# Float16 stacks with a per-row scale for the masked scores, and stacks of two head pairs on chip

## The chip, the cores and the metric

The kernel runs on one core of one Trainium2 chip. The metric is the device time of one execution in microseconds (us): the median of the runs of a kernel. The profile shows one execution, taken by the hardware profiler.

## The reference

The input is `q`, `k`, `v` of 4 batches, 8 heads, 768 rows and 64 columns, a projection of 64x6, and the weights of a two-layer block (512 to 2048 to 512). Cut to what matters:

```python
q_bucket = sum over n of (q @ proj[:, n] > 0) * 2**n        # 6 bits, and the same for k
mask     = q_bucket[:, :, :, None] == k_bucket[:, :, None, :]
scores   = where(mask, (q @ k^T) / 8, -1e9)                  # 768 x 768 for each head
attn     = exp(scores - rowmax); attn /= rowsum + 1e-9
x        = (attn @ v), heads side by side                    # 3072 x 512
h        = maximum(x @ w_in, 0)
out      = (h * h) @ w_out
```

## The kernel before

**Units and visits.** A unit is 128 rows of scores of one head against all 768 keys; there are 192 units (lines 840 to 848). A visit is six units: one half (384 rows) of a pair of heads, three units of each head. There are 32 visits, eight for each batch. The first eight visits (batch 0, 48 units) are "plain": their scores are one product of float32 stacks. The other 144 units (batches 1 to 3) work with two products of float32r stacks, and these are the ones that the change touches.

**Stacks.** `prep` (line 582) makes the operands of one pair of heads. `R` is loaded with 64 rows of k above 64 rows of q. A projection gives `pd`, the sign of it the bits (`bits`, ScalarE), and a small matmul turns these into bit patterns (`pc`). `A` is `R` rounded to float32r, with q scaled by 1/8; `L` is the rest that the rounding left out. Five DMAs from SBUF to SBUF on SP's queue (`send`) rearrange the halves, so that the first product (`Q` with `A`) and the second (`M` with `L`) add up, in PSUM, to the full-precision score and to the mask: the bit rows lie in `M`, with values of the order of 2^100, so that a row whose bits differ falls out of the exponential. Each of `A`, `L`, `Q`, `M` is 128x768 of 4 bytes in two buffers (line 37). A pair of heads takes one buffer of each for each head, so both buffers are taken by one pair, and a head of the next pair waits until the same head of the pair before has been read for the last time.

**One unit** (line 671). TensorE writes four score matmuls into `pS` (two products, two halves of 384 columns). From unit 36 on `pS` has one place in PSUM only: every second unit before that uses the space of `po` (line 674). VectorE takes the negated row maximum `nmx` (line 682). ScalarE writes `e = exp(pS + nmx)` with the row sum `sm` (line 685). Then `rv = 1/(sm + 1e-9)` (VectorE or GpSimd, then a reciprocal on VectorE), `hl` is `e * rv` split into two float16 parts (the high part mostly on ScalarE, the low part on VectorE), a DMA transpose writes `aT`, and `av` (line 709) multiplies it with the values, `pA`. `pS` comes free for the next unit when the exponential has read it.

**The two-layer block** (`moe`, line 732) runs for each half batch as soon as its four visits are done: 16 steps `f` with 12 matmuls `pm` (384 columns) and 9 matmuls `po` (512 columns) each. ScalarE and VectorE turn `pm` into the two float16 parts of `g`. It is what TensorE has to do beside the units.

**The order** of all instructions is made by a list scheduler in the kernel itself (`Program.order`, line 238): every operation is recorded with its cost (line 188), the scheduler runs forward and backward a few times, and the result is what each engine executes in order. `rank` is its first priority. `PACE` (line 64) holds the matmuls of the two-layer block back: the step number m may not start before the unit that is read off between the points (unit, step), so that at unit 193 step 640 of 896 is allowed. All instructions are issued by one helper, so that nearly all have line 420 (and 417 for grouped matmuls) in the profile; one goes by the tiles' names.

Of the kernel before, what the change touches and what calls it, by code (L numbers as in the profile page):

```python
# [30 lines left out]
NF = DFF // P  # L31
BIG = float(2.0**100)
SC = 0.125
ASC = float(2.0**14)


# [24 lines left out]
WIN_AT, WOUT_AT = (0, 2), 1  # L61
FIRST = len(WIN_AT)

PACE = ((25, 0), (64, 120), (193, 640))

IDLE_FROM, IDLE_SHARE = 1000, 0.6

# [55 lines left out]
class Program:  # L123
# [35 lines left out]
    def add(self, *ways):  # L159


        ways = [w for w in ways if w[0].key != "pool" or not any(isinstance(x, View) and x.rec.kind == "psum" for x in w[2])]
        queue, name, args, kw = ways[0]
        if name == "matmuls":
            used = [(x, n == 0) for a, _ in args for n, x in enumerate(a)]
        else:
            used = [(args[0], True)] + [(x, False) for x in args[1:]] + [(x, k == "accum_out") for k, x in kw.items()]
        used = [(x.rec, w, self.region(x)) for x, w in used if isinstance(x, View)]
        i, deps = len(self.ops), set()
        for rec, w, (p0, p1, f0, f1, fs, g0, g1) in used:  # L170
            if rec.before is not None:
                deps |= rec.before.ops
            for j, w2, (a0, a1, b0, b1, bs, c0, c1) in rec.accesses:
                if (w or w2 or rec.kind == "psum") and a0 < p1 and p0 < a1 and b0 < f1 and f0 < b1 and not (fs and fs == bs and (c1 <= g0 or g1 <= c0)):
                    deps.add(j)
        for rec, w, r in used:
            rec.ops.add(i)
            rec.accesses.append((i, w, r))
        deps.discard(i)
        if self.mark is not None:  # L180
            self.paced.append((i, self.mark))
        behind = () if name == "matmuls" or not name.startswith("dma") or queue.key != "sp" else self.first
        self.ops.append(Op([w + (self.cost(w[0].key, *w[1:]), self.port(w[0].key, *w[1:])) for w in ways], deps, self.rank))
        if i not in behind:
            self.ops[i].after |= set(behind)

    @staticmethod
    def cost(key, name, args, kw):

        size = lambda x: int(np.prod(x.shape[1:]))  # L190
        column = {F32: 4 / 2.4, F32R: 0.445}
        if name == "matmuls":

            side = {32: 4, 64: 2}.get(size(args[0][0][1]), 1)
            t = sum(size(a[2]) * column.get(a[2].dtype, 1 / 2.4) + 7 for a, _ in args) / side
            return t, t
        kinds = [x.rec.kind if isinstance(x, View) else "" for x in args]
        ptr = any(isinstance(x, View) and x.shape[-1] == 1 for x in args[2:3])
        n = max(size(args[0]), size(args[1]) if isinstance(args[1], View) else 0)
        if key == "pe":  # L200
            if "is_transpose" in kw:
                return 110, 110
            t = max(107, size(args[2]) * column.get(args[2].dtype, 1 / 2.4) + 3)
            return t, t
        if name.startswith("dma"):
            b = int(np.prod(args[0].shape)) * mybir.dt.size(args[0].dtype)
            inside = name == "dma_start_transpose" or kinds[:2] == ["sb", "sb"]
            busy = 1040 if key == "pool" else (650 if inside else 475) + 50 * (key == "act")
            return busy, b / (TRANSPOSES if name == "dma_start_transpose" else 314)
        if key == "act":  # L210
            t = 93 * (isinstance(kw.get("scale"), View) + isinstance(kw.get("bias"), View)) + (51 if "psum" in kinds[:2] else 93) + n / 1.2 + 93 * ("accum_out" in kw)
        elif key == "pool":
            t = 147 + n * (2.1 if args[0].dtype == F32 or args[0].dtype == F32R else 1.88) if name == "tensor_tensor" else 161 + n / 1.2 + 83 * ptr
        else:
            fast = name in ("tensor_copy", "tensor_scalar") and "psum" not in kinds[:2]
            both = len(args) > 3 and isinstance(args[3], View) and args[3].shape[-1] == 1
            t = 67 + n / (1.92 if fast else 0.96) + 62 * (ptr and (fast or name == "scalar_tensor_tensor")) + 100 * both
        return t, t
# [8 lines left out]
    @staticmethod  # L227
    def port(key, name, args, kw):

        if name.startswith("dma") or key not in ("dve", "pool"):  # L230
            return False
        ins = [x for x in args[1:] if isinstance(x, View) and x.shape[-1] > 1]
        inside = all(x.rec.kind == "sb" for x in ins)
        if key == "pool":
            return any(x.rec.kind == "sb" for x in args[1:] if isinstance(x, View) and len(x.shape) > 1 and x.shape[-1] > 1)
        return inside and (len(ins) == 2 or name in ("tensor_copy", "tensor_scalar"))
# [157 lines left out]
    def emit(self):  # L394
        info = mybir.DependencyInfo(mybir.DependencyClass.NoSync, mybir.DependencyReason.DATA)
        last = {}
        def issue(q, ins):
            if q.key in last:
                self.tc.add_manual_dep(ins, last[q.key], info, reason="in order")
            last[q.key] = ins.name  # L400
        out = self.order()
        fill, end = {}, IDLE_FROM
        for i in out[: out.index(self.busy_from)]:
            o = self.ops[i]
            if o.queue is self.pe:
                if o.start > end + 300:
                    fill[i] = int((o.start - end) * IDLE_SHARE / 56)
                end = o.start + o.busy
        for i in out:
            o = self.ops[i]  # L410
            q = o.queue
            for _ in range(fill.get(i, 0) if self.idle[1].rec.tile is not None else 0):
                issue(q, q.engine.matmul(self.idle[0].real(), self.idle[1].real(), self.idle[1].real(), start=True, stop=True).ins)
            real = lambda x: x.real() if isinstance(x, View) else x
            if o.name == "matmuls":
                for args, kw in o.args:
                    ins = q.engine.matmul(*map(real, args), **kw).ins  # L417
                    issue(q, ins)
                continue
            ins = getattr(q.engine, o.name)(*map(real, o.args), **{k: real(x) for k, x in o.kw.items()}).ins  # L420
            issue(q, ins)

# [10 lines left out]
def lsh_attention_moe(ctx: ExitStack, tc, kq, v, proj2, w_in, w_out, consts, out):  # L433
# [27 lines left out]
    def sb(shape, dtype, name, bufs=1, tag=None):  # L461
        return pr.tile(sbp, "sb", shape, dtype, name, BUFS.get(tag or name, bufs), tag)
# [116 lines left out]
    def matmuls(*args, start=True, stop=True):  # L579
        pr.add((pe, "matmuls", [(a, {"start": start, "stop": stop}) for a in args], {}))  # L580

    def prep(b, hp, plain):
        r0 = pr.rank
        Rs, Rqs = [], []
# [14 lines left out]
        matmuls(*[(pd[32 * n : 32 * n + 32], pj, Rs[n // 2][:, n % 2 * HS : (n % 2 + 1) * HS]) for n in range(4)])  # L599
        bits = sb([P, HS], BF16, "bits")  # L600
        act.activation(bits, pd, AF.Sign, scale=2.0**60, bias=thr)
        out = []
        for odd, R in enumerate(Rs):
            pr.rank = r0
            if plain:
                M = sb([P, S], F32, "M" if odd else "L")
            else:

                A, L, Q, M = [sb([P, S], F32R, name) for name in "ALQM"]
                move(A, R, cst[:, 2:3])  # L610
                left(L, R, cst[:, 2:3], f32(A))
            pr.rank = r0 + STACKS
            if not plain:
                send(f32(Q[T]), f32(A[U]))
                send(f32(Q[U]), f32(L[U]))
                send(f32(A[U]), f32(A[T]))
            for half in range(2):
                w = slice(half * HS, (half + 1) * HS)
                n = 2 * odd + half
# [3 lines left out]
            if plain:  # L623

                move(R[U], M[T], 1.0, HALVES if r0 > 0 else (act, dve))
                move(M[T], Rqs[odd], SC)
                out.append(((M, R),))
            else:
                send(f32(L[U]), f32(M[T]))
                send(f32(M[T]), f32(Q[T]))  # L630
                out.append(((Q, A), (M, L)))
        return out

    vscales, loaded = {}, {}
# [36 lines left out]
    def unit(st, half, i, aT, plain):  # L671
# [6 lines left out]
            for j in range(2):  # L678
                pe.matmul(pS[:, j, 0:HS], a[:, c0 : c0 + P], bb[:, j * HS : (j + 1) * HS], start=s == 0, stop=s == len(st) - 1)
        sS = pS[:, 0:2, 0:HS]  # L680
        nmx = sb([P, 1], F32, "nmx", 2)
        dve.tensor_reduce(nmx, sS, AX.XY, ALU.max, negate=True)
        e = sb([P, S], F32, "e", BUFS["e"])
        sm = sb([P, 1], F32, "sm", 2)
        act.activation(e.rearrange("p (j s) -> p j s", j=2), sS, AF.Exp, bias=nmx, accum_out=sm)
        pr.rank = u
        rv = sb([P, 1], F32, "rv", 3)
        pr.add(*[(q, "tensor_scalar", (rv, sm, 1e-9, 1.0 if plain else 1.0 / ASC, ALU.add, ALU.mult), {}) for q in (dve, pool)])
# [35 lines left out]

    def unscaled(b, j=None):

        back = sb([P, 1], F32, "back", 16)
        dve.tensor_scalar(back, vscales[b][1], vscales[b][1], 2.0**46, ALU.mult, ALU.mult)
        dve.tensor_scalar(back, back, common if j is None else zs[:, j : j + 1], 1.0, ALU.mult, ALU.mult)
        return back  # L730
# [167 lines left out]
```

## Time and profile before

| what | us |
|---|---|
| median of 3 runs | 894.41 (893.44 to 894.41) |
| the profiled execution | 897.11 |
| its span in the profile | 895.3 |
| first and last exponential of the 144 float32r units | 193.7, 766.0 |
| last but one | 732.1 |

The span falls into four stretches. Up to 194 us the plain units run and the weights are split. From 194 to 732 us the 143 units of batches 1 to 3 run, with the two-layer block of the half batches before them. From 732 us on it is nearly the two-layer block alone, with one last unit at 766 us. In the tables of the profile PE is TensorE's matmuls, PEld its weight loads, DVE is VectorE, ACT ScalarE, POOL GpSimd. A group's row gives its busy time and the mean duration of one in ns; matmuls overlap in the pipeline, so the mean of one is longer than the time from one to the next. In a timeline a row stands for the first of its instructions, with start, time and count.

### The profile page before, as it was taken

How to read it: one execution, taken by the hardware profiler on the slowest of the kernel's cores; microseconds unless marked ns; L12 is line 12 of the kernel's file. 1: busy time of each engine (PE TensorE's matmuls, PEld its weight loads, DVE VectorE, ACT ScalarE, POOL GpSimd, SP SyncE). 2: the span in 40 equal slices, each digit the busy share in tenths (PEclk: the TensorE clock that was granted, in tenths of full speed). 3: DMA queues.
4: the chain of work that ended last, by engine and by line, in shares of the span. 5: the costliest groups of instructions: out<-in, count | busy, mean ns of one | idle time of the engine just before them, and what ended most of it. 6: DMA issues, size and time to landing. Idle time of an engine off the chain costs nothing.

```text
span 895.3 us, 14201 instructions
## 1 busy us (share of the span) xinstructions
PE 860.8 (96%) x5082; PEld 478.9 (53%) x5082; DVE 612.0 (68%) x1149; ACT 641.3 (72%) x1180; POOL 110.5 (12%) x159
## 2 busy tenths in 40 slices
PE   7997988999999999999999999999999999999997
PEld 5553543455555555555555555555555555555553
DVE  5888888989888677888776768887767661211111
ACT  4877786889798778798777868877778773533433
POOL 2663653300220000100000000000000000000000
PEclk9998997999999999999999999999999999999999
DMA  7548549787989897999898968897979740200000
GB/s 239 174 127 170 169 154 236 160 176 150 209 180 205 140 203 132 221 186 211 153 216 151 201 125 186 171 183 130 184 146 202 146 89 17 73 1 1 36 0 36
DMA packets 279974, 131.82 MB, mean 147 GB/s; under 512 B 258272, under 2 KB 258400, under 8 KB 279904
## 3 DMA queue, kind: packets, MB, share of 16 engines
q1 hardware_dynamic: 279424, 130.91, 69.2%
q8 instruction: 40, 0.66, 0.3%
q14 instruction: 30, 0.25, 0.1%
q10 hardware_dynamic: 480, 0.01, 0.0%
HBM read 37.30 MB, written 6.29 MB: 49 GB/s over the span
## 4 chain that ended last, share of the span: by engine, by line
PE 46%; DMA 2%; ACT 2%; DVE 2%; issue 1%; SPq 0%; ACTq 0%
PE po L420 18%; PE pm L420 17%; PE pS L420 6%; PE pA L417 5%; DMA M<-Q 1%; ACT o L420 1%; DVE nmx L420 1%; ACT g L420 1%; ACT hl L420 0%; DMA L<-M 0%; DMA Q<-L 0%; PE pd L417 0%; DVE hl L420 0%; ACT e L420 0%; PE pc L420 0%
## 5 line engine op out<-in xcount | busy, mean ns | idle before, releaser
L420 PE MATMUL pm<-xx,win 128*128 128x384 f16 x1536 | 330.2, 328 | 1.8 <-ACT g L420 1.6
L420 PE MATMUL po<-wo,g 128*128 128x512 f16 x1152 | 330.0, 380 | 0.9 <-ACT o L420 0.8
L420 DVE TENSOR_REDUCE nmx<-pS 128x1 f32<-128x768 f32 x192 | 183.1, 953 | 54.3 <-PE pS L420 52.0
L420 ACT ACTIVATE e<-pS,nmx 128x768 f32<-128x768 f32 x192 | 172.0, 896 | 64.0 <-DVE nmx L420 59.1
L420 PEld LDWEIGHTS <-win 128*128 128x128 f16 x1536 | 145.7, 98 | 119.2 <-issue 20.6
L420 DVE SCALAR_TENSOR_TENSOR hl<-e,rv,hl 128x768 f16<-128x768 f32 x162 | 164.6, 1018 | 30.0 <-ACT hl L420 29.7
L420 PEld LDWEIGHTS <-g 128*128 128x128 f16 x1152 | 107.5, 98 | 127.5 <-issue 21.6
L420 ACT ACTIVATE hl<-e,rv 128x768 f16<-128x768 f32 x157 | 145.3, 929 | 24.3 <-ACT e L420 12.1
L420 DVE SCALAR_TENSOR_TENSOR g<-g,g 128x384 f16<-128x384 f32 x122 | 67.5, 554 | 129.1 <-ACT g L420 128.3
L420 ACT ACTIVATE g<-pm 128x384 f32<-128x384 f32 x125 | 60.8, 486 | 103.3 <-PE pm L420 103.1
L420 ACT ACTIVATE g<-g 128x384 f16<-128x384 f32 (+1 forms) x251 | 130.4, 520 | 5.7 <-PE po L420 0.6
L420 PE MATMUL pS<-A,Q 128*128 128x384 f32 x288 | 93.1, 403 | 5.7 <-ACT e L420 5.7
L417 PE MATMUL pA<-aT,VV 128*64 128x384 f16 x972 | 91.6, 329 | 0.0
L420 POOL TENSOR_SCALAR rv<-sm 128x1 f32<-128x1 f32 x71 | 27.3, 384 | 482.1 <-ACT e L420 480.3
L420 PE MATMUL pS<-L,M 128*128 128x384 f32 x288 | 76.5, 346 | 1.6 <-DMA M<-Q 1.6
L417 PEld LDWEIGHTS <-VV 128*64 128x64 f16 x972 | 49.4, 109 | 37.7 <-issue 19.7
L420 PEld LDWEIGHTS pS<-A,Q 128*128 128x128 f32 x288 | 47.4, 189 | 34.0 <-ACT e L420 20.7
L420 PEld LDWEIGHTS pS<-L,M 128*128 128x128 f32 x288 | 51.5, 188 | 5.3 <-issue 3.2
L420 PE MATMUL pS<-Q,M 128*128 128x384 f32 x96 | 39.3, 526 | 4.6 <-ACT e L420 4.6
L420 PE MATMUL pS<-A,L 128*128 128x384 f32 x96 | 38.8, 519 | 4.2 <-ACT e L420 4.2
L420 DVE TENSOR_SCALAR rv<-sm 128x1 f32<-128x1 f32 x121 | 18.3, 151 | 32.1 <-ACT e L420 29.0
L420 DVE TENSOR_SCALAR M<-pc,cst 128x384 fp32r<-128x384 f32 (+1 forms) x56 | 37.6, 671 | 2.5 <-PE pc L420 2.4
(111 smaller groups left out, 679.5 us busy)
## 6 DMA issues: line engine op xcount, KB each, us to landing
R<-kq SPq DMA_DIRECT2D x24, 384.0 KB
raw<-w_in SPq DMA_DIRECT2D x16, 511.8 KB
raw<-w_out SPq DMA_DIRECT2D x16, 511.8 KB
V<-vp SPq DMA_DIRECT2D x16, 384.0 KB
out<-o SPq DMA_DIRECT2D x21, 256.0 KB
Q<-L SPq DMA_DIRECT2D x24, 192.0 KB
Q<-A SPq DMA_DIRECT2D x24, 192.0 KB
A<-A SPq DMA_DIRECT2D x24, 192.0 KB
```

The source lines that it names most:

```text
L417: ins = q.engine.matmul(*map(real, args), **kw).ins
L420: ins = getattr(q.engine, o.name)(*map(real, o.args), **{k: real(x) for k, x in o.kw.items()}).ins
```

## The change

Stacks are float16. For each pair of heads a new function `bounded` finds from the sums of squares of `R` (two ScalarE squares with accumulated sums, a small matmul `pn`, nine small VectorE operations) a power of two for k and q, `own`, by which `A` is scaled before it is rounded to float16, and `exact`, the factor that turns the product back. The mask values become 49152 in place of 2^100, which `cst` and `sgn` are rescaled for once. The exponential then has a scale for each row: `exact`, or 0 for a row whose maximum tells that no key has the same bits. So for each of the 144 units VectorE runs two more operations on 128x1 behind the row maximum, in one piece (`chain`), and the exponential reads its scale and its bias from SBUF.

`A` and `Q` of a head are now the halves of one tile of 128x2x768 float16, `L` and `M` those of another; the first head of a pair takes the tags `A` and `L`, the second `Q` and `M`. A tile has the bytes of one before, each tag still has two buffers, and a pair of heads takes one buffer of each, so that two pairs are on chip. The five DMAs for each head move half the bytes. `PACE` allows step 680 at unit 193, and `back` has 12 buffers in place of 16.

```diff
-PACE = ((25, 0), (64, 120), (193, 640))
+PACE = ((25, 0), (64, 120), (193, 680))
...
+            if o.name == "chain":
+                for name, args, kw in o.args:
+                    issue(q, getattr(q.engine, name)(*map(real, args), **{k: real(x) for k, x in kw.items()}).ins)
+                continue
...
+    def bounded(Rs):
+
+        if not halved:
...
+            dve.tensor_scalar(cst[:, 0:2], cst[:, 0:2], fac, 1.0, ALU.mult, ALU.mult)
...
+        sums = sb([P, 2], F32, "sums")
+        for n, R in enumerate(Rs):
+            act.activation(sb([P, S], BF16, "sqk", tag="sqv"), R, AF.Square, accum_out=sums[:, n : n + 1])
+        for n, h in enumerate((T, U)):
+            dve.tensor_scalar(few[h, 2 * n : 2 * n + 2], sums[h], 2.0**120, 1.0, ALU.min, ALU.mult)
+        pn = ps([P, 512], F32, "pn", tag="misc")[:, 0:4]
+        pe.matmul(pn, ones, few, start=True, stop=True)
+        both = sb([P, 8], F32, "both")
+        size, flip = both[:, 0:4], both[:, 4:8]
+        dve.tensor_scalar(size, pn, 2.0**8, 2.0**120, ALU.max, ALU.min)
+        dve.tensor_scalar(u32(size), u32(size), 1, 0x7F800000, ALU.logical_shift_right, ALU.bitwise_and)
+        dve.tensor_scalar(u32(flip), u32(size), 0x7F800000, 0x7F800000, ALU.bitwise_xor, ALU.bitwise_and)
+        found = sb([P, 4], F32, "found", 4)
+        own, exact = found[:, 0:2], found[:, 2:4]
+        for n, h in enumerate((T, U)):
+            dve.tensor_scalar(own[h], flip[h, 2 * n : 2 * n + 2], 2.0**-51, 1.0, ALU.mult, ALU.mult)
+        dve.tensor_scalar(size, size, 2.0**50, 1.0, ALU.mult, ALU.mult)
+        dve.scalar_tensor_tensor(exact, size[:, 0:2], SC, size[:, 2:4], ALU.mult, ALU.mult)
+        return own, exact
...
-                A, L, Q, M = [sb([P, S], F32R, name) for name in "ALQM"]
-                move(A, R, cst[:, 2:3])
-                left(L, R, cst[:, 2:3], f32(A))
+                A, Q, L, M = [x[:, n] for x in (sb([P, 2, S], F16, name) for name in ("AL", "QM")[odd]) for n in range(2)]
+                to = own[:, odd : odd + 1]
+                move(A, R, to)
+                left(L, R, to, A)
...
-        nmx = sb([P, 1], F32, "nmx", 2)
-        dve.tensor_reduce(nmx, sS, AX.XY, ALU.max, negate=True)
+        line = sb([P, 3], F32, "line", 2)
+        nmx, bias, scale = [line[:, n : n + 1] for n in range(3)]
+        todo = [("tensor_reduce", (nmx, sS, AX.XY, ALU.max), {"negate": True})]
+        if len(st) > 1:
+            todo += [("tensor_scalar", (scale, nmx, MASK * MASK / 2, factor[st[1][0].rec], ALU.is_lt, ALU.mult), {}),
+                     ("tensor_scalar", (bias, nmx, scale, 1.0, ALU.mult, ALU.mult), {})]
+        pr.add((dve, "chain", todo, {}))
...
-        act.activation(e.rearrange("p (j s) -> p j s", j=2), sS, AF.Exp, bias=nmx, accum_out=sm)
+        to = {"bias": bias, "scale": scale} if len(st) > 1 else {"bias": nmx}
+        act.activation(e.rearrange("p (j s) -> p j s", j=2), sS, AF.Exp, accum_out=sm, **to)
```

The scheduler makes a new order from this. Two places show what it does to the engines that wait for each other.

TensorE at the first unit of the eighth of the twelve pairs in batches 1 to 3, before (`pS` are the scores, `pm` and `po` the two-layer block, `win` and `g` its weights as they are loaded; a float32r matmul holds its weight load in one row):

```order
L420 MATMUL pS<-A,Q 128x384 x2
L420 LDWEIGHTS win
L420 MATMUL pm<-xx,win 128x384
L420 LDWEIGHTS win
L420 MATMUL pm<-xx,win 128x384
L420 LDWEIGHTS g
L420 MATMUL po<-wo,g 128x512
L420 LDWEIGHTS g
L420 MATMUL po<-wo,g 128x512
L420 MATMUL pS<-L,M 128x384 x2
```

The same place in the changed kernel:

```order
L430 MATMUL pm<-xx,win 128x384
L430 LDWEIGHTS A
L430 MATMUL pS<-A 128x384
L430 LDWEIGHTS A
L430 MATMUL pS<-A 128x384
L430 LDWEIGHTS L
L430 MATMUL pS<-L 128x384
L430 LDWEIGHTS L
L430 MATMUL pS<-L 128x384
L430 LDWEIGHTS win
L430 MATMUL pm<-xx,win 128x384
```

Before, the second product of the unit stood behind four matmuls of the two-layer block, since its stacks were late; now the four score matmuls stand together.

VectorE at one unit before (from one row maximum to the next):

```order
L420 TENSOR_REDUCE nmx<-pS 128x1
L420 SCALAR_TENSOR_TENSOR hl<-e,rv,hl 128x768
L420 TENSOR_SCALAR rv<-sm 128x1
L420 RECIPROCAL rv<-rv 128x1
L420 TENSOR_REDUCE nmx<-pS 128x1
```

And at the same unit of the changed kernel:

```order
L428 TENSOR_REDUCE line<-pS 128x1
L428 TENSOR_SCALAR line<-line,found 128x1
L428 TENSOR_SCALAR line<-line 128x1
L430 SCALAR_TENSOR_TENSOR hl<-e,rv,hl 128x768
L430 TENSOR_SCALAR rv<-sm 128x1
L430 RECIPROCAL rv<-rv 128x1
L428 TENSOR_REDUCE line<-pS 128x1
```

The two operations that make the row's scale and bias stand between the row maximum and everything behind it, the low part of `hl` of the unit before among it; the exponential waits for the second of them.

More of the change, by code (lines that the diff above doesn't have):

```diff
@@ L33 @@
 SC = 0.125
+MASK = 49152.0
 ASC = float(2.0**14)
@@ L165, in add @@
             used = [(x, n == 0) for a, _ in args for n, x in enumerate(a)]
+        elif name == "chain":
+            used = [(x, n == 0) for _, a, _ in args for n, x in enumerate(a)]
         else:
@@ L191, in cost @@
         column = {F32: 4 / 2.4, F32R: 0.445}
+        if name == "chain":
+            t = sum(Program.cost(key, *x)[0] for x in args)
+            return t, t
         if name == "matmuls":
@@ L228, in port @@
     def port(key, name, args, kw):
-        if name.startswith("dma") or key not in ("dve", "pool"):
+        if name == "chain" or name.startswith("dma") or key not in ("dve", "pool"):
             return False
@@ L580, in matmuls @@
         pr.add((pe, "matmuls", [(a, {"start": start, "stop": stop}) for a in args], {}))
+    halved, factor = [], {}
+    few = sb([P, 4], BF16, "few")
+    dve.memset(few, 0.0)
+    def bounded(Rs):
+        if not halved:
+            fac = sb([P, 1], F32, "fac")
+            for h, x in ((T, MASK / BIG), (U, MASK)):
+                dve.memset(fac[h], x)
+            dve.tensor_scalar(cst[:, 0:2], cst[:, 0:2], fac, 1.0, ALU.mult, ALU.mult)
+            w = sgn.rearrange("p (n t c) -> p n t c", n=4, t=2)
+            for t, x in ((0, MASK / BIG), (1, MASK)):
+                dve.tensor_scalar(w[:, :, t], w[:, :, t], x, 1.0, ALU.mult, ALU.mult)
+            halved.append(True)
+        sums = sb([P, 2], F32, "sums")
[17 more added lines that the diff above has]
+        return own, exact
     def prep(b, hp, plain):
@@ L601, in prep @@
         act.activation(bits, pd, AF.Sign, scale=2.0**60, bias=thr)
+        if not plain:
+            own, exact = bounded(Rs)
         out = []
@@ L607, in prep @@
             else:
-                A, L, Q, M = [sb([P, S], F32R, name) for name in "ALQM"]
-                move(A, R, cst[:, 2:3])
-                left(L, R, cst[:, 2:3], f32(A))
+                A, Q, L, M = [x[:, n] for x in (sb([P, 2, S], F16, name) for name in ("AL", "QM")[odd]) for n in range(2)]
+                to = own[:, odd : odd + 1]
+                move(A, R, to)
+                left(L, R, to, A)
             pr.rank = r0 + STACKS
             if not plain:
-                send(f32(Q[T]), f32(A[U]))
-                send(f32(Q[U]), f32(L[U]))
-                send(f32(A[U]), f32(A[T]))
+                send(Q[T], A[U])
+                send(Q[U], L[U])
+                send(A[U], A[T])
             for half in range(2):
@@ L628, in prep @@
             else:
-                send(f32(L[U]), f32(M[T]))
-                send(f32(M[T]), f32(Q[T]))
+                send(L[U], M[T])
+                send(M[T], Q[T])
                 out.append(((Q, A), (M, L)))
+                factor[M.rec] = exact[:, odd : odd + 1]
         return out
@@ L725, in unscaled @@
     def unscaled(b, j=None):
-        back = sb([P, 1], F32, "back", 16)
+        back = sb([P, 1], F32, "back", 12)
         dve.tensor_scalar(back, vscales[b][1], vscales[b][1], 2.0**46, ALU.mult, ALU.mult)
```

## The prediction

> **What bounds the kernel now.** I read the page first, for the engines' shares over the span.
>
> ```profile
> PE 860.8 (96%) x5082; PEld 478.9 (53%) x5082; DVE 612.0 (68%) x1149; ACT 641.3 (72%) x1180; POOL 110.5 (12%) x159
> PEclk9998997999999999999999999999999999999999
> ```
>
> TensorE is busy 96% of the span, at a granted clock of nearly 1 after the first stretch. The table by stretches says where the other engines have room:
>
> ```profile
> 0.00:194.00 194.00, 174.83 (x942) 96.58 (x943) 164.38 (x343) 142.63 (x279) 87.63 (x120) 0.96 0.69 182
> 194.00:300.00 106.00, 101.19 (x635) 56.92 (x634) 87.93 (x154) 89.44 (x153) 11.62 (x15) 1.00 0.88 178
> 300.00:732.00 432.00, 427.72 (x2632) 243.24 (x2630) 330.81 (x602) 342.36 (x620) 11.25 (x24) 1.00 0.89 171
> 732.00:895.30 163.30, 157.08 (x878) 82.16 (x875) 28.91 (x52) 66.91 (x131) 0.00 (x0) 0.99 0.08 23
> ```
>
> The columns are PE, PEld, DVE, ACT and POOL (busy us, instructions), clock, DMA share, GB/s. From 194 to 732 us, where the units of batches 1 to 3 run, TensorE is idle 4.8 + 4.3 = 9.1 us. VectorE is busy 418.7 of 538 us (78%), ScalarE 431.8 (80%). So time goes away only if TensorE gets less work or waits less, and it comes if TensorE waits more. Of the waits between 194 and 732 us these bear on TensorE (total us, times, longest):
>
> ```profile
> PEld pS L420 <- ACT e L420: 20.7, 53, 2.0
> PE pS L420 <- ACT e L420: 5.7, 7, 1.6
> PE pS L420 <- DMA M<-Q: 1.6, 4, 0.8
> PEld pS L420 <- DMA M<-Q: 1.2, 1, 1.2
> ```
>
> Nearly all is one wait: the scores of a unit wait until the exponential of the unit before has read `pS`, which has one place. A weight load that waits can be covered by a matmul that still runs, so 26.4 us is the upper bound of this stall and 9.1 us of idle time a lower one. The timeline shows the loop where it is tight:
>
> ```profile
> 715.34 0.15 DVE L420 TENSOR_SCALAR rv<-sm 128x1 f32<-128x1 f32 x1
> 715.36 0.61 PE L420 MATMUL pS<-A,Q 128*128 128x384 f32 x2 [0.33 <-ACT e L420]
> 715.53 0.16 DVE L420 RECIPROCAL rv<-rv 128x1 f32<-128x1 f32 x1
> ...
> 716.36 0.96 DVE L420 TENSOR_REDUCE nmx<-pS 128x1 f32<-128x768 f32 x1 [0.67 <-PE pS L420]
> ...
> 717.39 0.88 ACT L420 ACTIVATE e<-pS,nmx 128x768 f32<-128x768 f32 x1
> ...
> 718.42 0.47 PE L420 MATMUL pS<-A,Q 128*128 128x384 f32 x1
> ```
>
> Scores at 715.36, row maximum 1.00 us later, exponential at 717.39, the next scores at 718.42: 3.06 us. With 0.70 us for the four score matmuls (below), TensorE needs 2.36 us of other work between the scores of two units, or it waits.
>
> **Score matmuls.** One place where four float32r matmuls stand between a `po` and a `pm`, and the rates of other work from the chain that ended last:
>
> ```profile
> 469.65 0.38 PE L420 MATMUL po<-wo,g 128*128 128x512 f16 x1
> ...
> 470.57 0.34 PE L420 MATMUL pm<-xx,win 128*128 128x384 f16 x1
> ```
> ```profile
> 430.83 2.07 PE pA L417 x24
> ...
> 441.22 1.94 PE po L420 x9
> ...
> 460.18 1.95 PE pm L420 x12
> ...
> 473.75 1.10 PE pA L417 x12
> ```
>
> A `po` takes 1.94/9 = 0.215 us, a float16 matmul of 384 columns 1.95/12 = 0.1625. From the start of the `po` to that of the `pm` are 0.92 us, less 0.215 leaves 0.70 for the four scores. In float16 they are four of 0.1625, 0.65. That is 0.05 for each of 144 units: -7.2 us. So it buys little; one would expect more from the weight loads:
>
> ```profile
> L420 PEld LDWEIGHTS <-win 128*128 128x128 f16 x1536 | 145.7, 98 | 119.2 <-issue 20.6
> L420 PEld LDWEIGHTS pS<-L,M 128*128 128x128 f32 x288 | 51.5, 188 | 5.3 <-issue 3.2
> ```
>
> The Trainium skill (TensorE: Matmul & The Clock Gate, Back-to-back issue gap and Weight-path perf modes) says that the spacing of matmuls is set by load and matmul together, and that the fast weight load is for types other than FP32. By that rule four float32r scores would be spaced by the load, 4 x 0.188 = 0.75 us, the saving would be 14.7 us, and the sum below 896 us; the trace agrees on the loads (188 against 98 ns), not on the spacing (0.70).
>
> Of other work on TensorE: the new order has 51 runs of `pA` in place of 71, and a run costs 2 x 1.10 - 2.07 = 0.13 us for itself: -2.6. Twelve small `pn`, under 0.05 each: +0.5. The wait of the scores for the last stack (1.6 + 1.2 above) goes: -2.8. That wait was cheap because the scheduler had put other work there; in the order before, 15 score groups have 28 us of matmuls of the block inside them, where the second product's stacks are late, now 5 groups have 4 us. The chain before goes through such a place:
>
> ```profile
> 587.40 1.02 DVE L L420
> 588.44 4.09 DMA Q<-L
> 592.67 4.21 DMA L<-M
> 596.90 3.13 DMA M<-Q
> ```
>
> 12.5 us from `L` to the last of three transfers. With two pairs on chip this lies a pair ahead, and the halved transfers also relieve SP's queue. I book nothing for that beyond the 2.8, since TensorE was at work there.
>
> **The longer loop.** The nearest rows for two more operations on 128x1, one pointer each, and for an exponential that has a second pointer:
>
> ```profile
> L420 DVE TENSOR_SCALAR back<-fromv 128x1 f32<-128x1 f32 x11 | 2.0, 203 | 0.0
> L420 ACT ACTIVATE xx<-pA 128x384 f16<-128x384 f32 x27 | 13.0, 483 | 13.0 <-PE pA L417 13.0
> L420 ACT ACTIVATE xx<-pA,tov 128x384 f16<-128x384 f32 x4 | 2.3, 580 | 5.8 <-PE pA L417 5.8
> L420 ACT ACTIVATION_READ_ACCUMULATOR sqv<-V 128x1 f32 x16 | 3.0, 189 | 0.0
> L420 ACT ACTIVATE sqv<-V 128x768 bf16<-128x768 f32 x16 | 13.3, 833 | 3.3 <-DMA V<-vp 3.3
> ```
>
> A small operation with a pointer takes 0.203, and one that needs its predecessor's result starts 0.03 behind its end (`rv` ends at 715.49, the reciprocal starts at 715.53): 2 x 0.233 = 0.47. A pointer costs ScalarE 580 - 483 = 97 ns. So the loop grows by 0.56, and the work that TensorE needs between the scores of two units from 2.36 to 2.92 us. This stands in the loop, nothing hides it; queued behind the chain on VectorE are the low part of `hl`, `rv` and the reciprocal, and for them the DMA transposes wait.
>
> What TensorE has in these 143 gaps I summed from both orders at the rates above (`pm` 0.163, `po` 0.215, `pA` 0.082 and 0.2 for a run's start): 2.77 us in the mean before, 3.06 after, since 680 steps are allowed in place of 640 and the work inside score groups has moved into the gaps. Summing what is missing to a needed gap G over all gaps:
>
> | order | G, us | missing, us |
> |---|---|---|
> | before | 2.36 | 4.6 |
> | before | 2.61 | 15.4 |
> | after | 2.92 | 19.5 |
> | after | 3.17 | 37 |
>
> The tight loop alone gives 4.6 us before; what the trace has lies between 9.1 and 26.4. So gaps need about 0.25 more than the tight loop, since the row maximum or the exponential sometimes finds its engine at other work; 15.4 is near the middle, and I take it. With the same 0.25 the order after lacks 37 us: +21.5. The bounds: +4 (no more waiting than the tight loop) and, with twice the 0.25, about +48. The change to the scheduler's order moves the first score of batch 1 behind 6.6 us more of the block; that is work done earlier, not more of it, and costs nothing while TensorE is the bound. The end after the last unit keeps its work within 2 us.
>
> **Other engines.** `bounded` adds two squares for each pair, 24 x (0.83 + 0.19) = 24.5 us of ScalarE, and with the pointer 144 x 0.097 = 14 us: 431.8 becomes 470. VectorE gets 144 x 0.47 = 68 us and twelve times nine small operations (about 0.15 each, 16 us): 418.7 becomes 502. In a stretch of about 550 us that is 91% where it was 78%. Both have room; it is what the 0.25 rests on.
>
> **The sum.** -7.2 - 2.6 + 0.5 - 2.8 + 21.5 = +9.4. The profiled execution took 897.1 with a span of 895.3, 2.7 above the median, and the difference carries over: 894.4 + 9.4 = 903.8 us. About 0.2% (1.8 us) is what a measurement of this kernel can tell from no change.
>
> **The rivals.** (A) Faster: what delays the row maximum and the exponential by 0.25 is the crowding of stack work behind each pair's end (as at 587 us), and it goes when stacks are made a pair ahead. Then only the tight loop is missing, 19.5 - 15.4 = +4.1, the sum is -8.0 and the time 886. For it: the 15 split score groups, all but gone in the order. Against it: VectorE has more to do than before, and the waits of 194 to 732 us lie mostly between pairs' ends. It decides from a gap of 3.05 us downwards. Chance 0.30. The Trainium skill (Perfetto Trace Analysis, Optimization Strategy) says that a recurring gap on the engine that should be saturated can mean too few buffers; by that rule the second pair on chip is the remedy, and here the place that recurs in the waits is `pS`, which the change leaves at one. (B) No change: half of the 0.25 stays, 27 us missing, +12 against -12, 894. Chance 0.11. (C) VectorE becomes the bound: 502 us of work and half of the idle time that its order forces on it now, (538 - 418.7)/2 = 60, make a stretch of 562, less the 6.6 us that the new order does ahead of it 555, in place of 538: +17, with nothing of the saving on TensorE left to see, 911, and 916 if the low parts of `hl` come late besides. It decides from some 95% on; against it speaks that the order leaves VectorE 9%. Chance 0.14. (D) That the stacks do not come earlier, because the longer chain in `bounded` (two squares, the sum over rows, nine small operations, about 4.5 us) eats the lead, would leave the 2.8 in place: 907; it lies within the forecast.
>
> **How the numbers follow.** The forecast, 897 to 910, has 0.45; A 0.30, B 0.11, C 0.14. Slower is the forecast and C, 0.59; faster is A, 0.30; B is 0.11. The range leaves out the ends: 881 (A, with some 5 us that a new order can win in the first 194 us, where TensorE is idle for 19 us) to 916 (C).
>
> **What would show it.** Right: four scores in 0.65 us and a tight loop near 3.6 us; the wait of the scores for the exponential at 45 us or more in place of 26.4, that for `M` gone; TensorE's idle time between first and last unit up by some 20 us; VectorE at about 695 us in all, ScalarE at 680. Wrong: if the scores wait no longer than before although the loop is 0.56 longer, A holds; if the tight loop is shorter than 3.5 us, the operations on 128x1 cost less than their rows; if VectorE is busy over 95% of the stretch, C.

## The result, and the profile after

The changed kernel takes 903.21 us (median; 901.86 to 904.71 in 4 runs) against 894.14 before: a ratio of 1.0103, 95% interval 1.0086 to 1.0121. It is slower by 1.0%; 903.8 was predicted, with 881 to 916 as the range.

The page, busy times and slices:

```profile
span 902.9 us, 14665 instructions
PE 850.8 (94%) x5095; PEld 449.6 (50%) x5095; DVE 685.0 (76%) x1563; ACT 666.7 (74%) x1217; POOL 107.7 (12%) x158
```

TensorE is busy 10 us less than before, and the span is 7.6 us longer. VectorE has 73 us more work, ScalarE 25 us. The stretch that counts goes from the first score matmul of batch 1 to the exponential of the last unit but one. Before:

```profile
182.40:732.00 549.60, 540.51 (x3329) 306.43 (x3328) 429.92 (x790) 440.53 (x788) 22.86 (x39) 1.00 0.89 174
```

After:

```profile
187.40:763.00 575.60, 547.90 (x3433) 285.20 (x3433) 496.64 (x1170) 472.49 (x835) 23.12 (x42) 1.00 0.75 145
```

The first number is the stretch's length, the second TensorE's busy time in it: idle 9.1 us before, 27.7 after. Idle time is not all of the waiting: with the same 5095 matmuls in the same order, but without the two operations (first experiment below), TensorE is busy 840.9 us in place of 850.8, so waiting also adds to what the profile counts as busy. VectorE is busy 86% of the stretch where it was 78%, ScalarE 82% where it was 80%. The share of the DMA engines falls from 0.89 to 0.75. The loop where it is tight, after, in a timeline (a `pS` row stands for two matmuls):

```profile
453.92 0.48 PE L430 MATMUL pS<-Q 128*128 128x384 f16 x2
...
454.77 0.96 DVE L428 TENSOR_REDUCE line<-pS 128x1 f32<-128x768 f32 x1 [0.51 <-PE pS L430]
455.76 0.21 DVE L428 TENSOR_SCALAR line<-line,found 128x1 f32<-128x1 f32 x1
456.01 0.21 DVE L428 TENSOR_SCALAR line<-line 128x1 f32<-128x1 f32 x1
...
456.32 0.99 ACT L430 ACTIVATE e<-pS,line 128x768 f32<-128x768 f32 x1 [0.28 <-DVE line L428]
...
457.45 0.32 PE L430 MATMUL pS<-A 128*128 128x384 f16 x1
```

From scores to scores are 3.53 us, where they were 3.06. The row maximum ends at 455.73; the exponential, which started 0.07 us behind the maximum before, starts 0.59 us behind it, and takes 0.99 us in place of 0.88 to 0.90. The waits between 194 and 763 us:

```profile
ACT e L430 <- DVE line L428: 49.1, 62, 2.5
PE pS L430 <- ACT e L430: 19.3, 24, 2.8
DVE line L428 <- PE pS L430: 19.0, 42, 1.1
```

The matmuls' own wait for the exponential is 19.3 us where it was 5.7. The wait of weight loads cannot be compared, since a float16 weight load is recorded without `pS`: those of `A` and `Q`, the first of each unit, stood idle 41.4 us in this window with no releaser shown. So the 45 us or more that was to be a sign lies between 19.3 and 60.7, and cannot be read. No wait of the score matmuls for `M` or another stack is listed any more.

### The profile page after: what moved, and what is told of

It reads as the page before. It is cut to its first block, busy times and chain, and to the rows that moved or that the text cites. A ratio compares the mean times of both kernels' runs of the same rounds, so it can differ in the third digit from the quotient of the medians.

```text
span 902.9 us, 14665 instructions
## 1 busy us (share of the span) xinstructions
PE 850.8 (94%) x5095; PEld 449.6 (50%) x5095; DVE 685.0 (76%) x1563; ACT 666.7 (74%) x1217; POOL 107.7 (12%) x158
## 5 line engine op out<-in xcount | busy, mean ns | idle before, releaser
L430 PE MATMUL po<-wo,g 128*128 128x512 f16 x1152 | 324.4, 379 | 3.6 <-DVE g L430 1.5
L430 PE MATMUL pm<-xx,win 128*128 128x384 f16 x1536 | 322.6, 326 | 3.9 <-ACT g L430 2.8
L430 ACT ACTIVATE e<-pS,line 128x768 f32<-128x768 f32 x192 | 185.7, 967 | 65.1 <-DVE line L428 56.0
L428 DVE TENSOR_REDUCE line<-pS 128x1 f32<-128x768 f32 x192 | 182.7, 952 | 29.6 <-PE pS L430 27.7
L430 ACT ACTIVATE g<-g 128x384 f32<-128x384 f32 (+1 forms) x242 | 125.1, 519 | 5.1 <-PE po L430 0.4
L430 PE MATMUL pS<-A 128*128 128x384 f16 x144 | 35.0, 324 | 12.4 <-ACT e L430 11.9
L430 PE MATMUL pS<-Q 128*128 128x384 f16 x144 | 35.8, 325 | 7.9 <-ACT e L430 7.3
L430 ACT ACTIVATION_READ_ACCUMULATOR e<-pS,line 128x1 f32 x192 | 37.7, 196 | 0.0
L430 PE MATMUL pS<-M 128*128 128x384 f16 x144 | 35.4, 325 | 0.0
L430 PE MATMUL pS<-L 128*128 128x384 f16 x144 | 35.3, 325 | 0.0
```

The costliest lines, as they stand in the source:

```text
L428: issue(q, getattr(q.engine, name)(*map(real, args), **{k: real(x) for k, x in kw.items()}).ins)
```

## Experiments

Each kernel ran beside the kernel before on the same chip; the kernel before had medians of 894.91 (first four), 893.73 (next four) and 894.35 us (last two).

**The operations left out, order kept.** Every engine executes the changed kernel's order, without the two operations:

```diff
-                for name, args, kw in o.args:
+                for name, args, kw in o.args[:1]:
...
         to = {"bias": bias, "scale": scale} if len(st) > 1 else {"bias": nmx}
+        bias.alt, scale.alt = nmx, 1.0
```

> The changed kernel with every engine's order kept, but the two operations on 128x1 behind the row maximum are left out and the exponential takes the maximum as bias and 1.0 as scale (the row's scale and the rule for rows without a match are left out). Loop theory: the work needed between the scores of two units falls from 2.92 + 0.25 to 2.36 + 0.25 us, the gaps of this order then lack 10 us in place of 37, so 903.2 - 27 = 876 us (872 to 882), TensorE's wait for the exponential about a quarter of what it is. Rival, that VectorE's load sets it: about the same, 876, since its load goes as well. Rival, that the squares and small operations for each pair, or the new order itself, cost the time: 900 to 903.

Measured: 882.69 us, ratio to before 0.9859 (0.9832 to 0.9887). The operations and the pointer cost 20.5 us in the changed kernel; without them it would be faster than before by 1.4%. The squares, the small operations for each pair and the new order are not where the loss is. The size is 6.7 us short of the middle and the time 0.7 us above the upper end of what was expected. The matmuls' own wait for the exponential is 10.5 us (19.3 with the operations) where a quarter was expected. The trace shows a reason: the order had been laid out for the longer loop, and the exponential, free to start 0.07 us behind the maximum, starts 0.40 us behind it in the mean of 142 rounds; ScalarE is busy with other work for 0.35 of these.

**The operations run, but beside the loop.** As above, but both operations are issued at their place and write to a tile that nobody reads.

> The changed kernel with every engine's order kept and both operations on 128x1 still run by VectorE at the same place, but into a tile that nobody reads; the exponential takes the maximum as bias and 1.0 as scale and so waits for the maximum alone (the row's scale is left out). Loop theory: nearly all of the gain of the kernel without the operations, 876 to 883 us, since only the latency from maximum to exponential counted. Rival, that VectorE's load of 68 us more counts: 895 to 903.

Measured: 892.60 us, ratio 0.9976 (0.9961 to 0.9992). It is in neither theory's range. One place in its timeline shows that the exponential no longer waits for them:

```profile
459.85 0.96 DVE L429 TENSOR_REDUCE line<-pS 128x1 f32<-128x768 f32 x1
460.85 0.21 DVE L429 TENSOR_SCALAR dump<-line,found 128x1 f32<-128x1 f32 x1
460.89 0.88 ACT L431 ACTIVATE e<-pS,line 128x768 f32<-128x768 f32 x1
461.10 0.21 DVE L429 TENSOR_SCALAR dump<-line,dump 128x1 f32<-128x1 f32 x1
```

The exponential starts 0.08 us behind the maximum, while the first of the two operations runs. So of the 20.5 us, in this order, the way through the loop (both operations' latency and ScalarE's second pointer) is 10.6, from 903.2 to 892.6, and VectorE's time for the operations is 9.9, from 892.6 to 882.7. The stretch from the first score to the last unit but one, first with the operations beside the loop, then left out:

```profile
186.50:750.70 564.20, 542.75 (x3427) 286.38 (x3427) 493.77 (x1168) 458.17 (x836) 24.25 (x42) 1.00 0.77 148
```
```profile
185.90:740.40 554.50, 538.90 (x3427) 285.61 (x3427) 442.45 (x884) 457.95 (x836) 22.29 (x42) 1.00 0.78 151
```

The stretch is 575.6 us in the changed kernel, 564.2 with the operations beside the loop and 554.5 without them; TensorE is idle 27.7, 21.5 and 15.6 us of it. VectorE's 494 in place of 442 us make row maxima late although nothing waits for the operations themselves: in the mean of 142 rounds the maximum starts 0.48 us behind the start of the last score matmul without the operations, 0.59 with them beside the loop, 0.61 in the changed kernel. The share of the latency holds for this order alone. From the maximum's end to the exponential's start are 0.70 us in the mean in the changed kernel and 0.41 with the operations beside the loop, where 0.08 is possible; what an order made for the shorter way would win is not shown by this run.

**The kernel before with the operations.** Two operations and a second pointer in the old kernel, with float32r stacks, one pair and step 640, in values that change nothing:

```diff
+            todo += [("tensor_scalar", (scale, nmx, 2.0**120, unity, ALU.is_lt, ALU.mult), {}),
+                     ("tensor_scalar", (bias, nmx, scale, 1.0, ALU.mult, ALU.mult), {})]
```

> The kernel before with two operations on 128x1 behind the row maximum of the 144 units and a second pointer in the exponential, in values that change nothing; float32r stacks, one pair on chip and step 640 stay. Loop theory: its order has gaps of 2.85 us in the mean that lack 33 us to 2.92 and 56 us to 3.17, where before lacks 15, so 894.1 + 18 to 41, near 920 us. Rival, that the time was lost to the preparation of the float16 stacks: 894 to 897.

Measured: 941.15 us, ratio 1.0504 (1.0484 to 1.0524): 46 us slower, 5 more than the upper end. The direction settles it against the rival: the operations alone, without float16 stacks, make the old kernel slower.

```profile
PEld pS L429 <- ACT e L429: 68.8, 109, 2.7
...
PE pS L429 <- ACT e L429: 24.5, 40, 2.2
```

The scores' waits for the exponential, 26.4 us before (194 to 732 us), are 93.3 us here (194 to 760 us). The changed kernel, with the same operations, is 38 us faster. Step 680 is 11.7 us of that (next run); how the rest divides is not shown.

**Step 640.** `PACE` of the changed kernel back to `(193, 640)`.

> The changed kernel with step 640 in place of 680 at unit 193. Loop theory: the gaps have 2.94 us in the mean in place of 3.06 and lack 50 us to 3.17 in place of 37, so 903.2 + 13 = 916 us (908 to 920). Rival, that the pacing only moves work between the units and the end: 901 to 905.

Measured: 914.92 us, ratio 1.0221 (1.0201 to 1.0240): 11.7 us slower than the changed kernel, as the sum over the gaps had it (13).

**A true price for the scheduler.** `t = t if len(args) == 1 else 1367` in `cost`.

> The changed kernel with the scheduler told 1.37 us for the row maximum with its two operations, as the trace shows, in place of 1.16. Loop theory with its sum over the gaps: they lack 39 us to 3.17 in place of 37, ten runs of pA fewer save 1.3, so 904 us (899 to 908). Rival, that the scheduler's wrong price is what costs the time: 897 or less.

Measured: 905.55 us, ratio 1.0133 (1.0111 to 1.0155). A scheduler that knows the price gains nothing here. Why is not shown.

**One pair on chip.** Both heads of a pair take the tags `A` and `L`:

```diff
-(sb([P, 2, S], F16, name) for name in ("AL", "QM")[odd])
+(sb([P, 2, S], F16, name) for name in "AL")
```

> The changed kernel with float16 stacks, but the second head of a pair takes the same two tags as the first, so that one pair of heads is on chip as before. Loop theory: TensorE has other work when stacks are late, its gaps lack 31 us to 3.17 in place of 37, the wait for the last stack (2.8 us) comes back and ten more runs of pA cost 1.3: 901 us (897 to 906). Rival, that a second pair on chip is worth much because stack work crowds behind a pair's end: 912 us or more.

Measured: 900.15 us, ratio 1.0076 (1.0053 to 1.0099). The second pair of stacks on chip brings nothing; without it the kernel is 3 us faster, at the edge of noise.

**Balanced scales.** If the power of two for q is 1/8 of the inverse of that for k, the product is the score itself, and the exponential needs no scale. `bounded` finds that from the same norms; the masked scores, at -2.4e9, are so far below that a row without a match rounds to equal values.

```diff
+        dve.scalar_tensor_tensor(half, size[:, 2:4], SC, flip[:, 0:2], ALU.mult, ALU.mult)
+        dve.tensor_scalar(u32(half), u32(half), 1, 0x7F800000, ALU.logical_shift_right, ALU.bitwise_and)
+        dve.tensor_scalar(u32(back), u32(half), 0x7F800000, 0x7F800000, ALU.bitwise_xor, ALU.bitwise_and)
+        for h, x, to in ((T, half, 2.0**64), (U, back, SC * 2.0**-65)):
+            dve.tensor_scalar(own[h], x[h], to, 1.0, ALU.mult, ALU.mult)
...
-        to = {"bias": bias, "scale": scale} if len(st) > 1 else {"bias": nmx}
+        to = {"bias": nmx}
```

> The changed kernel, but the powers of two for k and q are chosen so that their product with the stacks is already the score (own for k about the root of the norms' ratio, own for q its inverse times 1/8), so that the exponential needs neither a scale nor the two operations behind the maximum; the scheduler plans anew. Loop theory: as with the order kept and the operations left out (882.7), the gaps lack 13 us to 2.61 where that order lacks 10, and ten more runs of pA: 885 us (878 to 890), below both kernels. Rival, that the float16 stacks bring nothing and what was won there came from the order alone: 893 to 897.

Measured: 882.49 us, ratio 0.9874 (0.9843 to 0.9904), below both kernels, as expected.

**Balanced scales, one pair on chip.**

> The kernel without row scales (balanced) with one pair of heads on chip. Loop theory: its gaps lack 9 us to 2.61 in place of 13, waits for the last stack come back (2.8): 884 us (880 to 890), the same as balanced. Rival, that the second pair on chip carries the gain: 893 us or more.

Measured: 871.25 us, ratio 0.9754 (0.9733 to 0.9774), the fastest version that keeps the search for the scales. That the second pair carries the gain is refuted; that it makes no difference is, too: without it, 11.2 us go, and the time is 9 us below the lower end of what was expected. The sum over the gaps had it 1 us faster. The row scales' price with one pair on chip is 28.9 us (900.15 against 871.25), with two 20.7 (903.21 against 882.49). In the stretch of the units, two pairs first:

```profile
182.30:737.30 555.00, 545.11 (x3443) 286.43 (x3443) 441.30 (x888) 455.58 (x835) 26.96 (x49) 1.00 0.78 150
```
```profile
178.60:728.90 550.30, 544.08 (x3447) 285.52 (x3447) 440.60 (x892) 458.54 (x840) 25.83 (x49) 1.00 0.77 151
```

TensorE is idle 9.9 and 6.2 us, and the stretch begins 3.7 us earlier with one pair. The spans of these two profiles, 877.3 and 868.9 us, differ by 8.4: 4.7 in the stretch, 3.7 ahead of it, where the scheduler's order is another. The granted clock over the whole run is 0.993 to 0.997 and 0.997 to 1.000 in the four runs of each; by their means that is some 3 us. Why it is so many microseconds is open; I made no run that keeps one order and changes only the buffers.

**Balanced, one pair, step 640.**

> The kernel without row scales and with one pair on chip (balanced_one_pair, 871.25), with step 640 in place of 680 at unit 193. Loop theory: with the short loop, too, the gaps must be filled; they have 2.77 us in the mean in place of 2.93 and lack 15 us to 2.61 in place of 9, so +6: 877.5 us (874 to 881). Rival, that pacing matters only where the loop is long: 870 to 873.

Measured: 881.98 us, ratio 0.9855 (0.9832 to 0.9877): 10.7 us slower than with step 680, where 6 were expected. The need for work in the gaps holds with the short loop; the size was off. This kernel also tells what float16 stacks bring without row scales: with one pair on chip and step 640 as in the kernel before, it differs from that by the stacks, the search for their scales and the buffers of `back`, and is 12.4 us faster (881.98 against 894.35).

**Balanced, one pair, constant scales.** The search for the scales (squares, small matmul, small operations) left out.

> As balanced_one_pair, but the powers of two are constants written once (1/4 for k, 1/2 for q): the two squares, the small matmul and the small operations for each pair are left out, so the finding of the scale from the norms is what this kernel leaves out. Loop theory: they stand beside other work, and this order's gaps lack 11 us to 2.61 in place of 9: 873 us (869 to 876). Rival, that VectorE's and ScalarE's load counts by itself, as the operations beside the loop suggest (10 us for 68 us of VectorE): some 16 us of VectorE and 25 us of ScalarE less, 866 us or less.

Measured: 870.23 us, ratio 0.9723 (0.9696 to 0.9749): 1 us less than with the search, which is not clear of noise. 25 us of ScalarE and, by its groups, 20 us of VectorE cost next to nothing there: they come once in 12 units and outside the loop. At the 9.9 us for some 60 us of the operations beside the loop, 20 us of VectorE would be 3 us, so a cost of that size is not ruled out.

## Why the prediction was right, step by step

**The bound and the forecast's mechanism.** TensorE is the bound and lost its time by waiting for scores: its idle time in the units' stretch rose by 18.6 us, predicted 21.5 - 2.8 = 18.7. Leaving out the operations takes 20.5 us off; putting them into the old kernel costs 46. The remaining terms sum to -12.1, and the changed kernel without the operations is 12.2 us faster than the kernel before (882.69 against 894.91). That both parts meet so closely is partly luck: two of the steps below were off, and their errors do not show in the sum.

**The loop.** 3.53 us, predicted 3.06 + 0.56 - 0.05 = 3.57. Between the two places shown, the way from the maximum to the exponential grew by 0.52 us and the exponential by 0.11, more than the 0.56 together; from the first score to the maximum it fell by 0.15 us (1.00 to 0.85), where 0.05 was predicted (see the scores below). The groups of the two operations after:

```profile
L428 DVE TENSOR_SCALAR line<-line 128x1 f32<-128x1 f32 x144 | 30.9, 214 | 5.0
L428 DVE TENSOR_SCALAR line<-line,found 128x1 f32<-128x1 f32 x144 | 30.8, 214 | 5.1
```

214 ns each where the nearest row gave 203, each 0.03 to 0.04 behind what it needs: 0.50 in place of 0.47. The second pointer costs 0.09 to 0.11 us, 0.097 predicted.

**The 0.25 us beside the tight loop: right in its sum, in part wrong in its cause.** I put all 21.5 us down to the loop's latency and took the delay by busy engines, 0.25, as unchanged. The operations beside the loop show that in this order the latency and the pointer are 10.6 us, and that VectorE's time for the operations is 9.9 by itself. So the step "with the same 0.25" does not hold for the operations: they also push the row maximum back, by 0.11 us in the mean, which I had kept for rival (C). Against the kernel before, the delay did stay the same in the mean of the rounds: the maximum starts 0.05 us later behind the last score (0.56 to 0.61), and the exponential's delay over what the chain needs fell by 0.04 (0.15 to 0.11). The new order made up for it, which I had not worked out; that is luck. VectorE is not the bound: it is busy 86% of the stretch. Its load counts where its queue stands in the loop; the VectorE time in `bounded`, outside the loop, costs 1 us together with 25 us of ScalarE.

**The scores.** Four float16 scores behind a run of `po`, after:

```profile
699.84 0.49 PE L430 MATMUL pS<-A 128*128 128x384 f16 x2
...
700.49 0.81 PE L430 MATMUL po<-wo,g 128*128 128x512 f16 x3
```

0.65 us from their start to that of the next `po`, as predicted. The 0.70 of float32r is right only where the scores follow other matmuls without a wait. Behind a wait for the exponential, before and after:

```profile
715.36 0.61 PE L420 MATMUL pS<-A,Q 128*128 128x384 f32 x2 [0.33 <-ACT e L420]
...
716.16 1.64 PE L420 MATMUL pm<-xx,win 128*128 128x384 f16 x9
```
```profile
718.98 0.48 PE L430 MATMUL pS<-A 128*128 128x384 f16 x2 [0.20 <-ACT e L430]
...
719.63 1.24 PE L430 MATMUL po<-wo,g 128*128 128x512 f16 x5
```

Four float32r scores take 0.80 us there, four of float16 0.65 again. In the kernel before some 33 of the 128 groups whose four matmuls stand together started late; at 0.10 us more for each, an estimate, the term -7.2 was some 3 us too small. The saving is more than spent by the waits. The rule of the Trainium skill (TensorE: Matmul & The Clock Gate, Back-to-back issue gap) by which load and matmul together set the spacing, so that here the longer loads would set it and the sum be 896, is not borne out where nothing waits: the float32r loads took 188 ns, and their matmuls 0.70/4 = 175. Behind a wait the mean is 0.80/4 = 200.

**The other terms.** The wait for `M` is gone (-2.8). The first score of batch 1 comes 5.0 us later (187.4 against 182.4; 6.6 us of the block ahead of it were predicted). VectorE has 685.0 in all, predicted 695, ScalarE 666.7, predicted 680: the scheduler moved work away from ScalarE, which I had not counted (it has 242 of its 251 conversions of `g` and 8 of its 12 of `wo`). Where VectorE's 10 us went I have not traced.

**The rivals.** (A), that crowded stack work makes the 0.25 and two pairs on chip take it away, is refuted: the time is not 886, and the changed kernel with one pair is 3 us faster, not slower. The 28 us of split score groups were places that the scheduler had filled; what they cost beyond the 2.8 us that I booked no run shows by itself. (B) did not come: no half of the waiting went. (C) is not true as it was put, since VectorE is not the bound, but its load is about half of the operations' price in this order. (D) did not come by its own sign, since the 2.8 us of waiting for `M` are gone from the profile; its time, 907, is too near the forecast to tell.

**What stays open.** The sum over the gaps came near for the pacing with the long loop (13 predicted, 11.7 measured) and for the true price (1 and 2.3). It was too large when the operations were left out (27 and 20.5), too small when they were put into the old kernel (41 at most, and 46), and bad between two orders with a short loop (-1 and -11; 6 and 10.7). The kernel before with step 680 alone was not run, so what the pacing is worth by itself in that kernel is not shown. A part of such a difference lies in the first 190 us, where each new order runs differently. In the kernel before the granted clock is 0.50 there in two places, 84.0 to 90.6 us and 142 to 152 us; in the six us ahead of each TensorE was busy 2.6 and 4.0 us. Compare the first stretch before with that of the fastest kernel with a search:

```profile
0.00:182.40 182.40, 163.23 (x880) 90.32 (x880) 153.19 (x309) 133.89 (x264) 87.63 (x120) 0.95 0.67 179
```
```profile
0.00:182.40 182.40, 167.30 (x919) 93.76 (x924) 159.52 (x351) 145.57 (x289) 83.39 (x115) 1.00 0.71 187
```

The granted clock is 0.95 and 1.00; 5% of 182 us are 9 us at most. Over the whole span, in the mean of the runs, it is about 0.994 and 0.999, which is some 4 us. How much of the 23 us between the kernel before and that one it explains was not tried.

## What to carry to other kernels

When one PSUM place is passed from matmul to reduction to activation and back, price the round trip, and compare it with the work that the matmul engine has in between: two operations on 128x1 cost 20 us here, and twenty-four squares of 128x768 with their small operations, outside the loop, 1 us. Before adding a correction for each row, see whether the operands can be scaled so that none is needed. A second buffer for something that is late is worth little where the bound engine has other work: here a second pair of stacks brought nothing.

## What the runs showed of the hardware

A small VectorE operation on 128x1 costs 214 ns with a pointer, and behind the one whose result it needs it starts 35 ns after that one's end; the exponential started 0.10 us behind the second (456.32 against 456.22). Half of the price of two such operations was, in the order kept, their place in VectorE's queue (9.9 of 20.5 us), though VectorE was idle 12% of the stretch with them beside the loop. Four float32r matmuls of 128x384 took 0.70 us behind other matmuls and 0.80 behind a wait; four of float16 took 0.65 in both places.
